# Top-k attention and a hardswish feed-forward: one reciprocal for two pairs of heads, keys and queries transposed by the DMA crossbar, shorter last chains

## The chip, the cores and the metric

The kernel runs on one core of a Trainium2 chip. The metric is device time in microseconds of that core, median of three runs. A core has TensorE (matmuls), VectorE, ScalarE and GpSimd, each with its own in-order stream of instructions, and SyncE (SP), whose queue issues nearly all DMAs. In the profile they are PE (PEld is its weight load), ACT for ScalarE, DVE for VectorE, POOL for GpSimd.

## The reference, cut to what matters

For 8 batches, 8 heads, 576 positions and heads of 64:

```python
scores = scale * q @ k.T
kth = np.partition(scores, -32, axis=-1)[..., -32:-31]
scores = np.where(scores >= kth, scores, -1e9)
attn = exp(scores - max); attn = attn / (sum(attn) + 1e-9)
x = (attn @ v)            # heads side by side: 4608 x 512
h = x @ w_in              # 512 -> 2048
out = (h * clip(h + 3, 0, 6) / 6) @ w_out
```

The two weights arrive as 64-bit floats. The kernel turns each into float32 from its low and high word (`lo`, `hi`).

## The kernel before, in words

**Pairs and duos.** Two heads form a `Pair` (128 partitions wide with keys or queries of both). Two pairs of one batch and one tile of 128 queries form a `Duo`, the unit of the main loop; its two pairs are u=0 and u=1. The 576 queries are four tiles of 128 and a rest of 64; a duo of the rest (`u.rest`, qt = J) has one row a partition and pair instead of two, so half the work. There are 80 duos in 8 batches, 10 a batch: 64 full and 16 rest duos.

**A duo's way.** `scores` (L200) multiplies on TensorE and ScalarE copies the result to SBUF (L233, L236). `top` (L243) finds the 32nd largest of each row on VectorE: four rounds of MAX8 (L250) and, but for the last, MATCH_REPLACE8 (L254). `shift` (L259, GpSimd) makes the bias of the exponential, `exp` (L268, ScalarE) masks with a Prelu, exponentiates with a running sum `den`, and adds EPS to it (L283). `inverse` (L285) is a reciprocal on VectorE. `weights` (L289, GpSimd) multiplies by it (L297) and splits the words of the float32 result into 16-bit halves (L306). `flip` (L309) transposes these by the DMA crossbar from SP. `join` (L314) puts the halves together again as eT (ScalarE for u=0, GpSimd for u=1, L318). `values` (L326) multiplies by the values on TensorE (L338), and `place` (L347) copies to xT on ScalarE.

**Feed-forward.** When both duos of a tile of queries are placed, `feed_forward` is queued (L442): a block of 128 tokens in 16 pieces, eight of matmuls with w_in (L365) with ScalarE's Relu and copy, and GpSimd's gate (L379, L380), then eight with w_out (L385).

**Order.** The schedule is written out by hand: each engine gets its instructions in program order. The main loop (L564) has eight slots for each duo, one search round of one pair in each, so VectorE's searches are the clock of the program. Dictionaries (`usual`, `behind`, `early`, `soon`, L532 to L545) say at which slot, counted from the duo's own first one, each part stands; what stands at 13 is emitted five slots into the next duo. After the parts, `piece` emits feed-forward pieces: one a slot while any are left, an eighth more from 24 and again from 48 left, and half of it in rest duos (L597). The loop runs three duos past the last search, and then what is left follows.

**Keys and queries.** `Pair.load` brings them in by six DMAs on SP. `Pair.transpose` (L171) makes nine transposes on TensorE into PSUM and four ScalarE copies (L179, L180, L183). The pairs of the next batch are loaded at slot 0 of duos 4 to 7 of a batch and transposed at slot 5 of duos 5 to 8.

**Weights.** `convert` (L96) handles one of 32 chunks of 128 x 512 numbers: DMA to `st`; ScalarE's Abs of the high word into `a` (L108) and a scaled copy of the low word into `y` (L111); GpSimd's clamp (L109); on VectorE a shift of `a` (L117) and the sign put into `y` (L118); GpSimd's integer sum of both (L123). `a` and `y` come from the pool "g" in SBUF, which feed-forward uses too. A chunk a slot is begun, so all of it lies in the first four duos.

Of the kernel before, what the change touches and what calls it, by code (L numbers as in the profile page):

```python
# [9 lines left out]
ALU = mybir.AluOpType  # L10
F32 = mybir.dt.float32
U32 = mybir.dt.uint32
I32 = mybir.dt.int32
U16 = mybir.dt.uint16
# [15 lines left out]
def kernel(  # L30
# [9 lines left out]
    nc = tc.nc  # L40
    P = nc.NUM_PARTITIONS
    B, H, S, D = q.shape
    DM, FF = moe_w_in.shape
    J = S // P
    JP = J * P
    R = S - JP
    NHP = H // 2
    NFC = FF // P
# [8 lines left out]
    kqpool = pool("kq", 14)  # L57
# [5 lines left out]
    gpool = pool("g", 8)  # L63
# [3 lines left out]
    ps_w = pool("ps_w", 3, space=PSUM)  # L67
# [25 lines left out]

    WC = 512

    def convert(dst, src):  # L96

        st = kqpool.tile([P, 2 * WC], U32, tag="kq", name="st")
        nc.sync.dma_start(st[:], src)
        yield
        words = st[:].rearrange("p (n two) -> p n two", two=2)
        lo, hi = words[:, :, 0], words[:, :, 1]
        a = gpool.tile([P, WC], F32, tag="g", name="a")
        y = gpool.tile([P, WC], F32, tag="g", name="y")
        nc.scalar.activation(a[:], hi.bitcast(F32), AF.Abs)  # L108
        nc.gpsimd.tensor_scalar(a[:], a[:], HI_MOST, HI_LEAST, ALU.min, ALU.max)  # L109

        nc.scalar.activation(y[:], lo, AF.Copy, bias=2.0, scale=2.0**-51)  # L111
        yield

        au, yu = a[:].bitcast(U32), y[:].bitcast(U32)
        nc.vector.tensor_scalar(au, au, 3, None, ALU.logical_shift_left)  # L117
        nc.vector.scalar_tensor_tensor(  # L118
            out=yu, in0=hi, scalar=0x80000000, in1=yu,
            op0=ALU.bitwise_and, op1=ALU.bitwise_or,  # L120
        )
        yield
        nc.gpsimd.tensor_tensor(  # L123
            dst.bitcast(I32), a[:].bitcast(I32), y[:].bitcast(I32), ALU.add
        )

    def weight_chunks():
# [11 lines left out]
    class Pair:  # L139
# [3 lines left out]
            self.b, self.hp = b, hp  # L143
            self.vm, self.vr, self.kr = vms[hp], vrs[hp], krs[b % 2 * NHP + hp]

        def load(self):
            h0 = 2 * self.hp
            t = self.landed = kqpool.tile([P, 2 * J + 1, 2, D], F32, tag="kq", name="landed")
            for i, src in enumerate((k, q)):
                for hh in range(2):  # L150
                    nc.sync.dma_start(
                        t[:, i * J : (i + 1) * J, hh, :],
                        src[self.b, h0 + hh, 0:JP, :].rearrange("(p j) d -> p j d", j=J),
                    )
                nc.sync.dma_start(
                    t[i * R : (i + 1) * R, 2 * J, :, :],
                    src[self.b, h0 : h0 + 2, JP:S, :].rearrange("h s d -> s h d"),
                )
# [12 lines left out]
        def transpose(self):  # L171
            kq = kqpool.tile([P, JP + S], F32, tag="kq", name="kq")
            self.kT, self.qT = kq[:, 0:JP], kq[:, JP : JP + S]
            ps = big()
            for j in range(2 * J + 1):
                rows = self.landed[:, j, :, :].rearrange("p h d -> p (h d)")
                nc.tensor.transpose(ps[:, j * P : (j + 1) * P], rows, ident[:])  # L177
            c0 = 2 * JP
            nc.scalar.copy(kq[:, 0:c0], ps[:, 0:c0])  # L179
            nc.scalar.copy(kq[:, c0 : c0 + R], ps[:, c0 + R : c0 + 2 * R])  # L180
            for hh in range(2):
                d = slice(hh * D, (hh + 1) * D)
                nc.scalar.copy(self.kr[d, hh, :], ps[d, c0 : c0 + R])  # L183

    class Duo:

# [81 lines left out]
        def exp(self, u):  # L268

            nt, m = self.nt, self.m[u]  # L270
            for t in range(nt):
                row = self.row(u, t)
                nc.scalar.activation(  # L273
                    row, row, AF.Prelu, bias=m[:, t, TOP_K - 1 : TOP_K], scale=-1.0, alpha=FLAT
                )
            for t in range(nt):
                row = self.row(u, t)
                nc.scalar.activation(  # L278
                    row, row, AF.Exp, bias=self.less[u][:, t : t + 1], scale=-scale / FLAT,
                    accum_out=self.den[:, u, t : t + 1],  # L280
                )
            d = self.den[:, u, 0:nt]
            nc.scalar.activation(d, d, AF.Copy, bias=EPS)  # L283

        def inverse(self, u):  # L285
            d = self.den[:, u, 0 : self.nt]
            nc.vector.reciprocal(d, d)  # L287

        def weights(self, u):  # L289

# [18 lines left out]
        def flip(self, u):  # L309
            t16 = self.t16[u] = kqpool.tile([P, 2 * (2 * J + 1), P], U16, tag="kq", name="t16")  # L310
            n = 2 * self.nb
            nc.sync.dma_start_transpose(t16[:, 0:n, :], self.e16[u][:, 0 : n * P])
# [34 lines left out]
        def place(self):  # L347
            nc.scalar.copy(*self.pv)  # L348
# [55 lines left out]
    duos = []  # L404
    for b in range(B):
        halves = [pairs[b][0:2], pairs[b][2:4]]
        for qt in range(J):
            duos += [Duo(h, qt) for h in halves]


            if qt == (0 if b == B - 1 else J - 1) and not 2 < b < B - 1:
                duos += [Duo(h, J) for h in halves]
            elif 2 < b < B - 1 and qt % 2 == 0:
                duos.append(Duo(halves[qt // 2], J))
    assert J == NHP == 4
    per_batch = 2 * J + 2
    ND = len(duos)
# [68 lines left out]
    def land(count=1):  # L486

        for _ in range(min(count, len(chunks))):
            c = convert(*chunks.pop(0))
            next(c)  # L490
            landing.append(c)

# [17 lines left out]
    def pair_at(m, first):  # L510

        b, at = divmod(m, per_batch)
        return pairs[b + 1][at - first] if b + 1 < B and 0 <= at - first < NHP else None

    first = pairs[0]
    first[0].load()
    land(2)
    first[1].load()
    first[0].transpose()
# [10 lines left out]


    usual = dict(  # L532
        shift0=3, exp0=4, inverse0=9, weights0=10, flip0=12, join0=15,
        shift1=7, exp1=8, inverse1=13, weights1=14, flip1=16, join1=19, values=22, place=23,
    )

    behind = dict(usual, values=25, place=26)
    early = dict(
        shift0=3, exp0=3, inverse0=4, weights0=4, flip0=5, join0=8,
        shift1=7, exp1=7, inverse1=8, weights1=8, flip1=9, join1=12, values=12, place=13,  # L540
    )
    soon = dict(
        shift0=3, exp0=3, inverse0=5, weights0=5, flip0=7, join0=10,
        shift1=7, exp1=7, inverse1=9, weights1=9, flip1=11, join1=14, values=16, place=17,
    )  # L545
    queued = {}
    for m in range(ND):
        for part, at in (early if m < 2 else soon if m >= ND - 2 else behind if per_batch <= m < ND - 4 else usual).items():
            queued.setdefault(8 * m + at, []).append((m, part))

    def parts(slot, late=None):

        for m, part in sorted(queued.get(slot, []), key=lambda x: x[1][:-1] != "shift"):
            if late is not None and (part[:-1] in ("inverse", "weights")) != late:
                continue
            if part == "values":
                values(m)
            elif part == "place":
                place(m)
            else:  # L560
                getattr(duos[m], part[:-1])(int(part[-1]))

    due = 0.0
    for m in range(ND + 3):  # L564
        u = duos[m] if m < ND else None
        for i in range(8):
            if u:
                u.top(i // 4, i % 4)
            if m < 4:
                parts(8 * m + i, False)  # L570
            convert_step()
            if m == 0 and i == 0:
                first[3].load()
            if m == 0 and i in (1, 2):
                first[i + 1].transpose()
            if i == (4 if m == 0 else 1) and m + 1 < ND:
                duos[m + 1].scores()
            if m < 4:
                parts(8 * m + i, True)
            else:  # L580
                parts(8 * m + i)
            if m == 0 and i in (1, 4):
                for p in duos[i // 4].pairs:
                    p.load_values()
            if i == 0:
                p = pair_at(m, 4)
                if p:
                    p.load()
            if i == 3 and u and u.pairs[0].b and 1 <= m % per_batch <= 2:
                for p in duos[m - 1].pairs:  # L590
                    p.load_values()
            if i == 5:
                p = pair_at(m, 5)
                if p:
                    p.transpose()

            due += ((left > 0) + (left >= 24) / 8 + (left >= 48) / 8) / (2 if u and u.rest else 1)  # L597
            piece(int(due))
            due -= int(due)
# [36 lines left out]
```

## Time and profile before

| | us |
|---|---|
| median of 3 runs | 1581.27 (1579.84 to 1582.78) |
| span of the profiled run | 1578.5 |
| busy: PE / DVE / POOL / ACT | 1456.9 / 1466.8 / 1144.5 / 1096.3 |
| MAX8, all (L250) | 816.4 |
| MATCH_REPLACE8, all (L254) | 635.5 |
| reciprocals (L287) | 24.6 in 160 |
| transposes of keys and queries on TensorE (L177) | 41.5 in 288 |

Busy time is the sum of the instructions' durations. Neighbouring instructions of VectorE overlap a little, so what one costs in the stream is read from the starts of its neighbours. In a row of groups stand line, engine, operation, output and input with shapes, count, busy time and mean duration in ns, and at the end the engine's idle time before them and what ended it. In the slices each digit is the busy share, in tenths, of a fortieth of the span. In the chain each line is start, duration, and what ran.

### The profile page before, as it was taken

How to read it: one execution, taken by the hardware profiler on the slowest of the kernel's cores; microseconds unless marked ns; L12 is line 12 of the kernel's file. 1: busy time of each engine (PE TensorE's matmuls, PEld its weight loads, DVE VectorE, ACT ScalarE, POOL GpSimd, SP SyncE). 2: the span in 40 equal slices, each digit the busy share in tenths (PEclk: the TensorE clock that was granted, in tenths of full speed). 3: DMA queues.
4: the chain of work that ended last, by engine and by line, in shares of the span. 5: the costliest groups of instructions: out<-in, count | busy, mean ns of one | idle time of the engine just before them, and what ended most of it. 6: DMA issues, size and time to landing. Idle time of an engine off the chain costs nothing.

```text
span 1578.5 us, 28787 instructions
## 1 busy us (share of the span) xinstructions
PE 1456.9 (92%) x10272; PEld 1039.0 (66%) x10272; DVE 1466.8 (93%) x3105; ACT 1096.3 (69%) x1865; POOL 1144.5 (73%) x1264
## 2 busy tenths in 40 slices
PE   5256799979999999998999999999999999999899
PEld 3153566567767777666777777776777767677675
DVE  6999999999999999999999999999999999999700
ACT  6675777777777777777776786777766787777621
POOL 4868687777867777867687777867687777767841
PEclk9568999989999999999999999999999999999999
DMA  8652543444344543545254543446244443533410
GB/s 236 159 181 45 113 83 81 94 91 97 76 90 89 101 83 76 101 85 119 55 106 76 97 89 82 93 93 116 57 96 87 98 88 74 103 65 68 83 22 14
DMA packets 450319, 144.49 MB, mean 92 GB/s; under 512 B 433280, under 2 KB 441472, under 8 KB 450176
## 3 DMA queue, kind: packets, MB, share of 16 engines
q1 hardware_dynamic: 450176, 142.65, 43.5%
q8 instruction: 81, 1.33, 0.3%
q14 instruction: 62, 0.51, 0.1%
HBM read 45.09 MB, written 9.44 MB: 35 GB/s over the span
## 4 chain that ended last, share of the span: by engine, by line
DVE 51%; PE 35%; POOL 5%; issue 3%; ACT 3%; DMA 1%; SPq 1%; POOLq 0%; ACTq 0%; DVEq 0%
DVE m L250 26%; DVE wk L254 22%; PE h L365 14%; PE acc L385 13%; PE pv L338 4%; PE big L232 3%; POOL e L306 1%; DVE y L118 1%; POOL sc L297 1%; DMA t<-e 1%; POOL eT L318 1%; DVE a L117 1%; PE big L177 1%; ACT sc L278 1%; ACT eT L318 1%
## 5 line engine op out<-in xcount | busy, mean ns | idle before, releaser
L250 DVE MAX8 m<-wk 128x8 f32<-128x576 f32 x864 | 613.1, 746 | 2.2
L385 PE MATMUL acc<-w_out,g 128*128 128x512 f32 x1152 | 516.9, 600 | 14.1 <-POOL g L380 14.1
L365 PE MATMUL h<-xT,w_in 128*128 128x128 f32 x4096 | 485.5, 279 | 17.3 <-ACT xT L348 17.3
L365 PEld LDWEIGHTS h<-xT,w_in 128*128 128x128 f32 x4096 | 475.0, 195 | 39.5 <-issue 18.2
L254 DVE MATCH_REPLACE8 wk<-m,wk 128x576 f32<-128x576 f32 x576 | 423.7, 742 | 0.0
L385 PEld LDWEIGHTS acc<-w_out,g 128*128 128x128 f32 x1152 | 213.6, 191 | 260.4 <-issue 238.6
L297 POOL TENSOR_SCALAR sc<-sc,den 128x576 f32<-128x576 f32 x288 | 213.8, 753 | 229.9 <-DVE den L287 222.7
L306 POOL COPY e<-sc 128x2304 uint16<-128x2304 uint16 (+1 forms) x192 | 320.3, 1678 | 10.2
L278 ACT ACTIVATE sc<-sc,shift 128x576 f32<-128x576 f32 x288 | 220.4, 769 | 40.5 <-POOL shift L266 37.7
L318 ACT COPY eT<-t 128x2304 uint16<-128x2304 uint16 (+1 forms) x82 | 215.9, 2632 | 37.9 <-DMA t<-e 35.3
L273 ACT ACTIVATE sc<-sc,m 128x576 f32<-128x576 f32 x288 | 210.1, 777 | 46.2 <-DVE m L250 46.0
L338 PE MATMUL pv<-eT,vm 128*64 128x128 f32 (+1 forms) x2560 | 164.0, 273 | 57.9 <-ACT eT L318 45.8
L254 DVE MATCH_REPLACE8 wk<-m,sc 128x576 f32<-128x576 f32 x288 | 211.8, 742 | 0.0
L318 POOL COPY eT<-t 128x2304 uint16<-128x2304 uint16 (+1 forms) x78 | 203.8, 2613 | 6.9 <-DMA t<-e 6.5
L338 PEld LDWEIGHTS pv<-eT,vm 128*64 128x64 f32 x2560 | 135.2, 141 | 109.3 <-ACT eT L318 49.7
L250 DVE MAX8 m<-sc 128x8 f32<-128x576 f32 x288 | 203.3, 742 | 2.4 <-ACT sc L236 2.4
L373 ACT ACTIVATE g<-h,three 128x512 f32<-128x512 f32 x144 | 98.5, 684 | 150.0 <-PE h L365 140.6
L380 POOL TENSOR_TENSOR g<-g,hs 128x512 f32<-128x512 f32 x144 | 185.0, 1285 | 12.1 <-POOL g L379 0.2
L233 ACT COPY sc<-big 128x2048 f32<-128x2048 f32 (+1 forms) x65 | 119.3, 1836 | 26.1 <-PE big L232 26.0
L232 PE MATMUL big<-kq 64*128 64x512 f32 x512 | 136.4, 653 | 0.0
L379 POOL TENSOR_SCALAR g<-g 128x512 f32<-128x512 f32 x144 | 89.2, 620 | 62.6 <-ACT g L373 52.4
L395 ACT ACTIVATE o<-acc 128x512 f32<-128x512 f32 x36 | 21.4, 595 | 106.6 <-PE acc L385 106.6
(47 smaller groups left out, 1113.1 us busy)
## 6 DMA issues: line engine op xcount, KB each, us to landing
landed<-in_k_dram SPq DMA_DIRECT2D x64, 128.0 KB, 3.0
landed<-in_q_dram SPq DMA_DIRECT2D x64, 128.0 KB, 3.0
st<-in_moe_w_in_dram SPq DMA_DIRECT2D x16, 512.0 KB, 5.1
vm<-in_v_dram SPq DMA_DIRECT2D x64, 128.0 KB, 2.3
st<-in_moe_w_out_dram SPq DMA_DIRECT2D x16, 512.0 KB, 6.6
out_dram<-o SPq DMA_DIRECT2D x32, 256.0 KB, 2.4
t<-e SPq DMA_TRANSPOSE x160, 4.6
landed<-in_k_dram SPq DMA_DIRECT2D x32, 32.0 KB, 2.8
```

Source lines behind the costliest of these rows:

```text
L232: nc.tensor.matmul(banks[:, 2 * i + hh, :], pr.qT[d, qs], pr.kT[d, :])
L250: nc.vector.max(self.m[u][:, t, 8 * r : 8 * r + 8], self.cur[t])
L254: nc.vector.match_replace(wk, self.m[u][:, t, 8 * r : 8 * r + 8], self.cur[t], LOWEST)
L273: nc.scalar.activation(row, row, AF.Prelu, bias=m[:, t, TOP_K - 1 : TOP_K], scale=-1.0, alpha=FLAT)
L278: nc.scalar.activation(row, row, AF.Exp, bias=self.less[u][:, t : t + 1], scale=-scale / FLAT, accum_out=self.den[:, u, t : t + 1],)
L297: nc.gpsimd.tensor_scalar(row, row, self.den[:, u, t : t + 1], 1.0, ALU.mult, ALU.mult)
L306: nc.gpsimd.tensor_copy(halves[:, :, to : to + c1 - c0], words)
L318: copy(eT[:, 0 : self.nb, :] .rearrange("p c q -> p (c q)") .bitcast(U16) .rearrange("p (x h) -> p h x", h=2), self.t16[u][:, 0 : 2 * self ...
L338: nc.tensor.matmul(pv[hh * D : (hh + 1) * D, u * w : (u + 1) * w], pr.vm[:, hh, c, :] if c < J else pr.vr[:, hh, :], rhs, start=(c == 0), ...
L365: nc.tensor.matmul(h[:, (f - f0) * P : (f - f0 + 1) * P], w_in[:, i, f * P : (f + 1) * P], xT[:, i, :], start=(i == 0), stop=(i == NHP - 1),)
L380: nc.gpsimd.tensor_tensor(g[:], g[:], hs[:], ALU.mult)
L385: nc.tensor.matmul(acc[:], gs[f // nf][:, f % nf * P : (f % nf + 1) * P], w_out[:, f, :], start=(f == 0), stop=(f == NFC - 1),)
```

## The change

It has five parts. **Start:** the first pair's queries are loaded from ScalarE's queue and not SP's. **Conversion:** for the first 16 weight chunks (`early`, those of w_in) the low words go to a PSUM tile, and VectorE reads them from there; its result `ys` is a new tile of "g". **Reciprocal:** in the usual order one reciprocal handles both pairs of a duo; adding EPS is a part of its own (`settle`), and u=0's weights, flip and join move to slots 13, 15 and 18, next to those of u=1. **Last chains:** the last six duos take a shorter order (`soon`), the last one a still shorter one (`last`), and the last batch's rest duos follow its second query tile instead of its first. **Keys and queries:** for batches 1 to 7 TensorE's transposes give way to a split into 16-bit halves on GpSimd, a crossbar transpose from SP and a join by ScalarE's copies, spread over slots of two neighbouring duos; their loads come a duo earlier. It is meant to take work off VectorE and TensorE and to bring the last feed-forward blocks forward.

```diff
-    def convert(dst, src):
+    def convert(dst, src, early):
...
-        y = gpool.tile([P, WC], F32, tag="g", name="y")
+        y = (
+            ps_w.tile([P, WC], F32, tag="w", name="yp")
+            if early
+            else gpool.tile([P, WC], F32, tag="g", name="y")
+        )
...
+        ys = gpool.tile([P, WC], F32, tag="g", name="ys") if early else y
...
-            out=yu, in0=hi, scalar=0x80000000, in1=yu,
+            out=ys[:].bitcast(U32), in0=hi, scalar=0x80000000, in1=yu,
...
-            for i, src in enumerate((k, q)):
+            for i, (src, eng) in enumerate(((k, nc.sync), (q, queue or nc.sync))):
...
+        def split(self):
+            self.e16 = kqpool.tile([P, 2 * (2 * J + 1) * P], U16, tag="kq", name="e16")
+            nc.gpsimd.tensor_copy(
...
+        def flip(self):
+            self.t16 = kqpool.tile([P, 2 * (2 * J + 1), P], U16, tag="kq", name="t16")
+            nc.sync.dma_start_transpose(self.t16[:], self.e16[:])
+        def join(self):
...
+            copy(kq[:, 0:c0], halves[:, :, 0:c0])
+            copy(kq[:, c0 : c0 + R], halves[:, :, c0 + R : c0 + 2 * R])
+            for hh in range(2):
+                d = slice(hh * D, (hh + 1) * D)
+                copy(self.kr[d, hh, :], halves[d, :, c0 : c0 + R])
...
+        def inverse(self, us):
+            d = self.den[:, us[0] : us[-1] + 1, 0 : self.nt]
+            nc.vector.reciprocal(d, d)
+        def settle(self, us):
+            d = self.den[:, us[0] : us[-1] + 1, 0 : self.nt]
             nc.scalar.activation(d, d, AF.Copy, bias=EPS)
...
-            if qt == (0 if b == B - 1 else J - 1) and not 2 < b < B - 1:
+            if qt == (1 if b == B - 1 else J - 1) and not 2 < b < B - 1:
...
-            c = convert(*chunks.pop(0))
+            c = convert(*chunks.pop(0), early=len(chunks) >= NFC)
...
-    first[0].load()
+    first[0].load(nc.scalar)
...
     usual = dict(
-        shift0=3, exp0=4, inverse0=9, weights0=10, flip0=12, join0=15,
-        shift1=7, exp1=8, inverse1=13, weights1=14, flip1=16, join1=19, values=22, place=23,
+        shift0=3, exp0=4, shift1=7, exp1=8, settle01=8, inverse01=13, weights0=13, weights1=14,
+        flip0=15, flip1=16, join0=18, join1=19, values=22, place=23,
     )
...
     soon = dict(
-        shift0=3, exp0=3, inverse0=5, weights0=5, flip0=7, join0=10,
-        shift1=7, exp1=7, inverse1=9, weights1=9, flip1=11, join1=14, values=16, place=17,
+        shift0=3, exp0=4, shift1=7, exp1=8, settle01=8, inverse01=10, weights0=10, weights1=11,
+        flip0=12, flip1=13, join0=15, join1=16, values=18, place=18,
     )
+    last = dict(
+        shift0=3, exp0=3, settle0=3, inverse0=5, weights0=5, flip0=7, join0=10,
+        shift1=7, exp1=7, settle1=7, inverse1=8, weights1=8, flip1=9, join1=11, values=11, place=11,
+    )
...
-        for part, at in (early if m < 2 else soon if m >= ND - 2 else behind if per_batch <= m < ND - 4 else usual).items():
+        if m < 2:
+            when = early
+        elif m == ND - 1:
+            when = last
+        elif m >= ND - 6:
+            when = soon
+        else:
+            when = behind if per_batch <= m < ND - 8 else usual
...
-                p = pair_at(m, 4)
+                p = pair_at(m, 3)
...
-            if i == 5:
-                p = pair_at(m, 5)
+            for at, first_at, part in ((2, 4, "split"), (5, 4, "flip"), (1, 5, "join")):
+                p = pair_at(m, first_at) if i == at else None
                 if p:
-                    p.transpose()
+                    getattr(p, part)()
```

In the order for the first two duos (`early`) the reciprocals stay separate, as in `last`.

More of the change, by code (lines that the diff above doesn't have):

```diff
@@ L123, in convert @@
         nc.gpsimd.tensor_tensor(
-            dst.bitcast(I32), a[:].bitcast(I32), y[:].bitcast(I32), ALU.add
+            dst.bitcast(I32), a[:].bitcast(I32), ys[:].bitcast(I32), ALU.add
         )
@@ L144, in __init__, with load @@
             self.vm, self.vr, self.kr = vms[hp], vrs[hp], krs[b % 2 * NHP + hp]
-        def load(self):
+        def load(self, queue=None):
             h0 = 2 * self.hp
             t = self.landed = kqpool.tile([P, 2 * J + 1, 2, D], F32, tag="kq", name="landed")
-            for i, src in enumerate((k, q)):
+            for i, (src, eng) in enumerate(((k, nc.sync), (q, queue or nc.sync))):
                 for hh in range(2):
-                    nc.sync.dma_start(
+                    eng.dma_start(
                         t[:, i * J : (i + 1) * J, hh, :],
@@ L154, in load @@
                     )
-                nc.sync.dma_start(
+                eng.dma_start(
                     t[i * R : (i + 1) * R, 2 * J, :, :],
@@ L183, in transpose, with copy @@
                 nc.scalar.copy(self.kr[d, hh, :], ps[d, c0 : c0 + R])
+        def split(self):
+            self.e16 = kqpool.tile([P, 2 * (2 * J + 1) * P], U16, tag="kq", name="e16")
+            nc.gpsimd.tensor_copy(
+                self.e16[:].rearrange("p (h x) -> p h x", h=2),
+                self.landed[:]
+                .rearrange("p j h d -> p (j h d)")
+                .bitcast(U16)
+                .rearrange("p (x h) -> p h x", h=2),
+            )
[3 more added lines that the diff above has]
+        def join(self):
+            kq = kqpool.tile([P, JP + S], F32, tag="kq", name="kq")
+            self.kT, self.qT = kq[:, 0:JP], kq[:, JP : JP + S]
+            halves = self.t16[:].rearrange("p (h c) q -> p h (c q)", h=2)
+            def copy(dst, src):
+                nc.scalar.copy(dst.bitcast(U16).rearrange("p (x h) -> p h x", h=2), src)
+            c0 = 2 * JP
+            copy(kq[:, 0:c0], halves[:, :, 0:c0])
[3 more added lines that the diff above has]
+                copy(self.kr[d, hh, :], halves[d, :, c0 : c0 + R])
     class Duo:
@@ L281, in exp @@
                 )
-            d = self.den[:, u, 0:nt]
+        def inverse(self, us):
[3 more added lines that the diff above has]
+            d = self.den[:, us[0] : us[-1] + 1, 0 : self.nt]
             nc.scalar.activation(d, d, AF.Copy, bias=EPS)
-        def inverse(self, u):
-            d = self.den[:, u, 0 : self.nt]
-            nc.vector.reciprocal(d, d)
         def weights(self, u):
@@ L538 @@
     early = dict(
-        shift0=3, exp0=3, inverse0=4, weights0=4, flip0=5, join0=8,
-        shift1=7, exp1=7, inverse1=8, weights1=8, flip1=9, join1=12, values=12, place=13,
+        shift0=3, exp0=3, settle0=3, inverse0=4, weights0=4, flip0=5, join0=8,
+        shift1=7, exp1=7, settle1=7, inverse1=8, weights1=8, flip1=9, join1=12, values=12, place=13,
     )
     soon = dict(
-        shift0=3, exp0=3, inverse0=5, weights0=5, flip0=7, join0=10,
-        shift1=7, exp1=7, inverse1=9, weights1=9, flip1=11, join1=14, values=16, place=17,
+        shift0=3, exp0=4, shift1=7, exp1=8, settle01=8, inverse01=10, weights0=10, weights1=11,
+        flip0=12, flip1=13, join0=15, join1=16, values=18, place=18,
+    )
+    last = dict(
+        shift0=3, exp0=3, settle0=3, inverse0=5, weights0=5, flip0=7, join0=10,
+        shift1=7, exp1=7, settle1=7, inverse1=8, weights1=8, flip1=9, join1=11, values=11, place=11,
     )
@@ L547 @@
     for m in range(ND):
-        for part, at in (early if m < 2 else soon if m >= ND - 2 else behind if per_batch <= m < ND - 4 else usual).items():
+        if m < 2:
[6 more added lines that the diff above has]
+            when = behind if per_batch <= m < ND - 8 else usual
+        for part, at in when.items():
             queued.setdefault(8 * m + at, []).append((m, part))
@@ L553, in parts @@
         for m, part in sorted(queued.get(slot, []), key=lambda x: x[1][:-1] != "shift"):
-            if late is not None and (part[:-1] in ("inverse", "weights")) != late:
+            if late is not None and (part[:7] in ("inverse", "weights")) != late:
                 continue
@@ L559, in parts @@
                 place(m)
+            elif part[:-1] in ("settle0", "inverse0"):
+                getattr(duos[m], part[:-2])((0, 1))
+            elif part[:-1] in ("settle", "inverse"):
+                getattr(duos[m], part[:-1])((int(part[-1]),))
             else:
```

## The prediction

> **What bounds the kernel now.** I read the page's busy totals first, then its slices, then the groups of VectorE, the chain, and the timeline around VectorE's last search.
>
> ```profile
> PE 1456.9 (92%) x10272; PEld 1039.0 (66%) x10272; DVE 1466.8 (93%) x3105; ACT 1096.3 (69%) x1865; POOL 1144.5 (73%) x1264
> ...
> PE   5256799979999999998999999999999999999899
> ...
> DVE  6999999999999999999999999999999999999700
> ```
>
> VectorE and TensorE are equally busy, but not at the same time: VectorE is full from the second slice on and has nothing in the last two, where TensorE is full. So the span is VectorE's stream up to its last search, and then a tail that TensorE runs.
>
> ```profile
> L250 DVE MAX8 m<-wk 128x8 f32<-128x576 f32 x864 | 613.1, 746 | 2.2
> ...
> L118 DVE SCALAR_TENSOR_TENSOR y<-st,y 128x512 uint32<-128x512 uint32 x32 | 30.2, 943 | 0.0
> ...
> L287 DVE RECIPROCAL den<-den 128x2 f32<-128x2 f32 x128 | 19.7, 154 | 7.2 <-ACT den L283 7.0
> ```
>
> The last column, idle time before a group, is almost nothing for the searches. From one duo's first MAX8 to the next is 19.40 us for all of the full duos after the fourth, within 0.1 except near the end, and 11.22 for a rest duo: VectorE waits for nobody. TensorE's scores of the last duo start at 1453.22, a little ahead of VectorE's place for them (second search round of the duo that began at 1452.12). So TensorE, though full, holds up no search.
>
> ```profile
> 1487.06 0.16 DVE L287 RECIPROCAL den<-den 128x2 f32<-128x2 f32 x1
> 1487.13 1.40 DVE L250 MAX8 m<-wk 128x8 f32<-128x576 f32 x2
> ...
> 1489.89 1.41 DVE L250 MAX8 m<-wk 128x8 f32<-128x576 f32 x2
> 1498.04 0.17 DVE L287 RECIPROCAL den<-den 128x2 f32<-128x2 f32 x1 [6.73 <-ACT den L283]
> ```
>
> VectorE's last search ends at 1491.3. A reciprocal lasts 0.16 but delays the next MAX8 by 0.07 only (1487.06 to 1487.13): that is its price in the stream.
>
> ```profile
> 1492.99 2.69 POOL eT L318
> 1495.68 0.04 issue
> 1495.72 2.24 PE pv L338 x20
> 1497.96 4.46 PE h L365 x32
> 1502.42 10.30 PE acc L385 x24
> 1512.72 2.33 PE pv L338 x40
> 1515.05 3.63 PE acc L385 x8
> 1518.68 14.29 PE h L365 x128
> 1532.97 13.74 PE acc L385 x32
> 1546.71 14.29 PE h L365 x128
> 1561.00 13.75 PE acc L385 x32
> ```
>
> This is the tail by the chain. One block of the feed-forward is 14.29 + 13.74 = 28.0 us in 16 pieces, so 1.75 a piece. From 1491.3 to the end are 87.2 us: 4.4 waiting for eT, 42 pieces, the values products, 3.9 for the last output.
>
> [...] L118 reads two SBUF tensors and takes 0.67 to 1.75 us for one shape. [...] after its 4.41 us of idle, 20 matmuls took 2.24, against 2.33 for 40 later. [...] SP takes 0.64 us per issue here.
>
> **The change, part by part.**
>
> Start: first queries go out on ScalarE's queue beside the keys. TensorE waits 1.05 us for them today (transposes of the keys end at 5.63, those of the queries begin at 6.67). At most 1.05 comes back, at least 0; I take 1.0, since two queues save 1.9 us of issue and ScalarE has only its table load until 8.0.
>
> Low words in PSUM, for 16 of the 32 chunks: L118 then reads one SBUF tensor, and no longer meets GpSimd. In the timeline seven of the first sixteen run over the undisturbed 0.68, by 5.5 us together. [...] Net -4.5; ends -7 and 0 (the blocked time may come back in L117, which took up to 1.79).
>
> One reciprocal a duo: 77 of 160 go. In some 62 full duos each is worth 0.07, so -4.3. In rest duos a search already waits for the result before it, and the reciprocal stands in that gap: 0. The waits for den ahead of the old ones, 9.3 less the 6.7 after the last search, were 2.6: -2.6.
>
> What it adds: u=0's weights move from slot 10 to 13, right ahead of u=1's. GpSimd then has 2 x (2 x 0.75 + 2.10) = 7.2 us in a row. Queued behind it is shift of the next duo's u=1 (0.45); ScalarE's Exp waits for that (1.9), and the next joint reciprocal waits for Exp, with all of VectorE's searches behind it. Before a full duo's reciprocal there is room. When the next duo is a rest duo with 1.40 us slots, 2 x 2.42 + 6 x 1.40 = 13.3 us are there, and 7.2 + 0.45 + 1.9 + a gate of 1.9 = 11.5 are needed; from rest to rest duo 11.2 against about 10.8. Those are 12 + 4 places, with margins of 0.4 to 3.6. The old waits at such spots were 0.9 and 1.4. Bounds 0 and 2.0 each; I take 0.3, so +5.
>
> Keys and queries by the crossbar, 28 pairs. TensorE loses nine transposes of together 1.15 us a pair: 32 us, which no search waited for and the tail does not contain (no transposes after batch 7 began). GpSimd gains the split, 28 x 2.10 (the row of the 2304-wide copy) = 59, to 1203 us. ScalarE: from the eT copies of 2304 (2.80) and 1536 (1.93) the same kind of copy costs about 2.5 for 2048, 0.34 for 128, so 3.5 a pair against today's 1.01 + 0.22 + 2 x 0.21 = 1.65: +52, to 1148. SP gets 28 transposes more beside 160, 2.7 us each on its queue, landing in 4.6. The join stands four slots (9.7 us) after the flip, and behind it on ScalarE only work that VectorE wants seven slots later (next scores). All of it lies beside the searches: 0, which is the weakest zero here.
>
> Tail: counting the pieces in program order from the slot after the last search, 42 are left before and 41 after: the rest duos go one qt later and the pacing rule is the same. But values of the last duo now stand at slot 11 instead of 16, with 37 pieces behind them. TensorE reaches them early and waits. Chain after the last search: Prelu, Exp and settle 3.5, reciprocal 0.2, weights 3.6, crossbar 4.6, GpSimd's eT 2.8: 15.0 with gaps. Then the 82.8 us from 1495.72 to the end, less 5 pieces and one values: 82.8 - 8.8 - 2.3 = 71.7. Tail 86.7, against 87.2. Within 84 and 92, as GpSimd's order in it turns out.
>
> Sum: -1.0 - 4.5 - 4.3 - 2.6 + 5 - 0.5 = -7.9; 1581.3 - 7.9 = **1573**.
>
> **Rivals.** (a) TensorE is the bound: it has 35% of the chain and is at 97% between 160 and 1480. Then its 32 us come off: 1549. Against it: VectorE's even 19.40. Chance 0.10. (b) The new waits eat the gain: at 0.8 each the 16 places cost 13, and 1581 stays. For it: the small margins. Chance 0.12. (c) Slower: 2.0 at each of the 16 places is 32 us, less 12.4 won, with the tail as it was: 1601; ScalarE and GpSimd, with 111 us more, could do this too through late scores. For it: GpSimd would be at some 80% of VectorE's stretch and works strictly in order. Against it: today its waits for den alone are 222.7 us idle. Chance 0.18. The forecast, waits of 0 to 0.5, has 0.60.
>
> **How the numbers follow.** Faster is the forecast and (a): 0.70; same is (b): 0.12; slower is (c): 0.18. Low end: no new waits (-5), early gain at its best (-2.5), tail 84 (-2.7), and some relief of (a): 1556. High end: waits of about 1.2 at each place, 1588. (a) at 1549 and the larger part of (c) stay out.
>
> **What would show it.** Last MAX8 near 1484; full duos 19.33 apart; [...] waits of den L287 about 5 us, all near rest duos; TensorE idle some 7 us ahead of the last values product, then 37 pieces; no transposes after batch 0. The forecast is wrong if full duos drift above 19.4, if MAX8 waits for the copies of scores, or if TensorE's pieces after the last search are far from 41.

## The result, and the profile after

The changed kernel takes 1604.95 us (1603.54 to 1608.86), the kernel before 1581.16 in the same runs: ratio 1.0154, 95% interval 1.0134 to 1.0174. It is slower by 23.8 us, where 8 us less had been forecast.

First the page's busy totals and VectorE's slices of the changed kernel:

```profile
PE 1441.3 (90%) x10020; PEld 1021.7 (64%) x10020; DVE 1458.7 (91%) x3028; ACT 1125.8 (70%) x1788; POOL 1193.1 (74%) x1292
...
DVE  6999989999999989999999999999999989989700
```

VectorE and TensorE have less to do than before, and the span is longer all the same: single slices of VectorE show an 8 where there was a 9. The waits of the changed kernel, for VectorE and then for ScalarE (who waited, for whom; us in total, times, longest), say what VectorE stands for:

```profile
DVE den L323 <- ACT den L327: 40.4, 14, 6.3
```

```profile
ACT sc L315 <- POOL shift L303: 211.3, 62, 11.3
```

The same two of the kernel before:

```profile
DVE den L287 <- ACT den L283: 9.3, 4, 6.7
```

```profile
ACT sc L278 <- POOL shift L266: 37.7, 26, 6.8
```

Read from the starts of the searches, the 23.2 us between the two profiled spans are these (rows up to the last search add to 20.3):

| | before | after | |
|---|---|---|---|
| first four duos | to 144.1 | to 136.6 | -7.5 |
| a full duo | 19.40 | 19.34 | 60 x 0.06 = -3.6 |
| waits of VectorE after them, up to the last search | 2.9 | 34.3 | +31.4 |
| last search ends | 1491.3 | 1511.8 | +20.5 |
| tail behind it | 87.2 | 89.9 | +2.7 |

Of the 34.3 us, 28.3 are in six rest duos (counted from 0): 5.1 in duo 9, 2.9 in 19, 4.2 in 29, 5.9 in 47, 6.3 in 67, 3.9 in 75. The last two duos have 2.7. The wait in duo 47, in order of time, first GpSimd's, then ScalarE's, then VectorE's lines of the changed kernel's timeline (start, duration, what; in brackets the idle time ahead and who ended it):

```profile
903.18 2.10 POOL L195 COPY e<-landed 128x2304 uint16<-128x2304 uint16 x1 [6.45 <-issue]
...
912.61 1.48 POOL L337 TENSOR_SCALAR sc<-sc,den 128x576 f32<-128x576 f32 x2
914.15 2.10 POOL L346 COPY e<-sc 128x2304 uint16<-128x2304 uint16 x1
916.23 1.48 POOL L337 TENSOR_SCALAR sc<-sc,den 128x576 f32<-128x576 f32 x2
917.77 2.10 POOL L346 COPY e<-sc 128x2304 uint16<-128x2304 uint16 x1
...
921.88 0.20 POOL L300 TENSOR_TENSOR shift<-m 128x2 f32<-128x2 f32 x1
```

```profile
913.32 1.44 ACT L310 ACTIVATE sc<-sc,m 128x576 f32<-128x576 f32 x2
922.43 0.77 ACT L315 ACTIVATE sc<-sc,shift 128x576 f32<-128x576 f32 x1 [7.67 <-POOL shift L303]
```

```profile
905.38 0.17 DVE L323 RECIPROCAL den<-den 128x4 f32<-128x4 f32 x1
...
924.32 0.18 DVE L323 RECIPROCAL den<-den 128x4 f32<-128x4 f32 x1 [5.90 <-ACT den L327]
```

The joint reciprocal at 905.38 frees the weights, but GpSimd, which stood still for 6.45 us ahead of the split (L195), has two gates, a shift and a join to do first and starts them 7.2 us later, at 912.61. They run for 7.2 us without a break; behind them come a gate and then shift at 921.88. ScalarE has done its Prelu long since and waits 7.67 for shift. Exp and settle take 1.9, and VectorE, whose slots are short in this rest duo, has been at its next joint reciprocal for 5.90 us.

The tail of the changed kernel on TensorE:

```profile
1522.91 1.09 PE L378 MATMUL pv<-eT,vm 128*64 128x128 f32 x16 [1.24 <-ACT eT L358]
1523.84 0.39 PE L378 MATMUL pv<-eT,vr 128*64 128x128 f32 x4
1528.83 1.98 PE L378 MATMUL pv<-eT,vm 128*64 128x128 f32 x16 [4.61 <-POOL eT L358]
```

TensorE waits for the last duo's eT with 37 pieces still behind it, 17.0 us after the last search.

### The profile page after: what moved, and what is told of

It reads as the page before. It is cut to its first block, busy times and chain, and to the rows that moved or that the text cites. A ratio compares the mean times of both kernels' runs of the same rounds, so it can differ in the third digit from the quotient of the medians.

```text
span 1601.8 us, 28114 instructions
## 1 busy us (share of the span) xinstructions
PE 1441.3 (90%) x10020; PEld 1021.7 (64%) x10020; DVE 1458.7 (91%) x3028; ACT 1125.8 (70%) x1788; POOL 1193.1 (74%) x1292
## 5 line engine op out<-in xcount | busy, mean ns | idle before, releaser
L405 PEld LDWEIGHTS h<-xT,w_in 128*128 128x128 f32 x4096 | 477.8, 196 | 66.5 <-ACT xT L388 37.1
L346 POOL COPY e<-sc 128x2304 uint16<-128x2304 uint16 (+1 forms) x192 | 320.4, 1679 | 10.2
L358 POOL COPY eT<-t 128x2304 uint16<-128x2304 uint16 (+1 forms) x78 | 203.7, 2611 | 61.1 <-DMA t<-e 56.2
L337 POOL TENSOR_SCALAR sc<-sc,den 128x576 f32<-128x576 f32 x288 | 212.8, 750 | 46.0 <-DVE den L323 44.8
L378 PE MATMUL pv<-eT,vm 128*64 128x128 f32 (+1 forms) x2560 | 167.9, 277 | 78.5 <-ACT eT L358 56.6
L378 PEld LDWEIGHTS pv<-eT,vm 128*64 128x64 f32 x2560 | 139.1, 143 | 128.9 <-ACT eT L358 67.2
L419 POOL TENSOR_SCALAR g<-g 128x512 f32<-128x512 f32 x144 | 88.8, 616 | 98.9 <-ACT g L413 90.1
L195 POOL COPY e<-landed 128x2304 uint16<-128x2304 uint16 x28 | 58.9, 2104 | 43.1 <-DMA t<-e 26.9
```

Source lines behind the costliest of these rows:

```text
L337: nc.gpsimd.tensor_scalar(row, row, self.den[:, u, t : t + 1], 1.0, ALU.mult, ALU.mult)
L346: nc.gpsimd.tensor_copy(halves[:, :, to : to + c1 - c0], words)
L358: copy(eT[:, 0 : self.nb, :] .rearrange("p c q -> p (c q)") .bitcast(U16) .rearrange("p (x h) -> p h x", h=2), self.t16[u][:, 0 : 2 * self ...
L378: nc.tensor.matmul(pv[hh * D : (hh + 1) * D, u * w : (u + 1) * w], pr.vm[:, hh, c, :] if c < J else pr.vr[:, hh, :], rhs, start=(c == 0), ...
L405: nc.tensor.matmul(h[:, (f - f0) * P : (f - f0 + 1) * P], w_in[:, i, f * P : (f + 1) * P], xT[:, i, :], start=(i == 0), stop=(i == NHP - 1),)
```

## The experiments

Theory W: shift stands in GpSimd's queue behind what the joint reciprocal has bunched there, and the searches wait for it through Exp and the next reciprocal. Rival X: the crossbar's extra work on GpSimd, ScalarE and SP makes the waits by itself. Rival T: the tail. Variants called W2 and J, and a rival L, came up on the way. A wait total below ("waits") is that of VectorE after the fourth duo and ahead of the last search; single waits under 0.3 us are left out. All ratios are against the kernel before.

**Separate reciprocals** (`e1`):

```diff
-        shift0=3, exp0=4, shift1=7, exp1=8, settle01=8, inverse01=13, weights0=13, weights1=14,
-        flip0=15, flip1=16, join0=18, join1=19, values=22, place=23,
+        shift0=3, exp0=4, settle0=4, inverse0=9, weights0=10, flip0=12, join0=15,
+        shift1=7, exp1=8, settle1=8, inverse1=13, weights1=14, flip1=16, join1=19, values=22, place=23,
```

(in `soon` alike, with u=0's at 4, 8, 8, 10 and 13).

> The changed kernel with the two reciprocals of a duo separate again and u=0's weights back at slot 10, all else as changed. Theory W (joint reciprocal: 7.2 us of weights stand on GpSimd ahead of the next duo's shift, Exp waits for it, and the next joint reciprocal holds the searches next to rest duos): of the 34 us of waits at den ahead of the last search nearly all go, so 1605 - 31 = 1574 (1568 to 1580). Rival X (the crossbar's extra work on GpSimd, ScalarE and SP makes the waits, whatever the order of the reciprocals): still above 1594. Rival T (the tail took the time): at most 3 us of the 24 are in the tail, so T would leave it above 1598.

1579.44 us, ratio 0.9993 (0.9985 to 1.0002), waits 4.1. The whole loss is undone with the crossbar, the PSUM words and the last chains still in. Its tail is 90.2. X and T fall as sole causes.

**The joint reciprocal alone** (`e2`), the changed `usual` in the kernel before:

> The kernel before with the joint reciprocal alone (settle at 8, reciprocal and u=0's weights at 13, flips at 15 and 16, joins at 18 and 19; its last two duos as before). W in its plain form: the waits at the pairs of rest duos (4 to 5 us each in four places) and at some single ones come with it, so 1581 + 15 to 25 less 3.6 for the cheaper reciprocals: 1592 to 1603. If waits need both the joint reciprocal and the crossbar's split on GpSimd: 1578 to 1588, with waits at the pairs of rest duos alone. X: 1578.

1582.78 us, ratio 1.0015 (1.0009 to 1.0022), waits 11.6. W in its plain form is too large by a factor of two to three: about a third of the waits come with the joint reciprocal, the rest needs something else of the change too. The third is rough: its runs spread from 1580.60 to 1586.62 us, and the profiled one, which gives the waits, took 1580.77.

**The crossbar alone** (`e3`), `split`, `flip` and `join` of keys and queries in the kernel before:

> The kernel before with keys and queries of batches 1 to 7 by the crossbar alone, its separate reciprocals kept. W: VectorE's stream is as before, 1576 to 1584. X: waits at den or at the copies of scores of 15 us and more, above 1595. If TensorE's 32 us had been on the path: 1549.

1580.51 us, ratio 0.9996 (0.9987 to 1.0005), waits 2.1. GpSimd at 1197.9 us busy, 53 more than before, costs VectorE nothing that shows, and TensorE's relief (1456.9 to 1431.2 us busy) brings nothing.

**Start and PSUM words alone** (`e4`):

> The kernel before with the first queries on ScalarE's queue and the low words of 16 chunks in PSUM, nothing else. The changed kernel's first four duos are 7.3 us shorter in all, so 1581 - 7 = 1574 (1572 to 1577); if the 7.3 us came from the new order of the parts instead, 1581.

1577.55 us, ratio 0.9974 (0.9966 to 0.9983): half of what was expected. Its groups on VectorE, the word step without and with PSUM (count, busy us, mean ns):

```profile
L124 DVE SCALAR_TENSOR_TENSOR y<-st,y 128x512 uint32<-128x512 uint32 x16 | 14.7, 918 | 0.0
L124 DVE SCALAR_TENSOR_TENSOR ys<-st,yp 128x512 uint32<-128x512 uint32 x16 | 10.8, 673 | 0.0
```

All sixteen from PSUM are undisturbed (0.673 us in the mean; in the changed kernel 0.67 to 0.68 each, though GpSimd was at work during twelve of them), and the first four duos end at 139.8, 4.3 earlier. In `e2` they end at 140.7, 3.4 earlier: there a wait of 3.3 for GpSimd's clamp (13.3 in all before, 10.2 in `e2`) is gone. So the 7.5 of the changed kernel are the words and the new order in about equal parts.

**The split's own buffer** (`e5`), in the changed kernel:

```diff
-    kqpool = pool("kq", 14)
+    kqpool = pool("kq", 13)
+    splitpool = pool("split", 1)
...
-            self.e16 = kqpool.tile([P, 2 * (2 * J + 1) * P], U16, tag="kq", name="e16")
+            self.e16 = splitpool.tile([P, 2 * (2 * J + 1) * P], U16, tag="split", name="e16")
```

> The changed kernel with one of the 14 buffers of the pool kq set apart for the 16-bit halves of keys and queries, so that GpSimd's split never has to wait for a crossbar transfer that still reads the buffer. Theory W2 (joint reciprocal and crossbar together: flips come late, the split stalls GpSimd on them, the weights then start late and shift behind them later still): the idle time ahead of the split (43 us) goes, waits at den fall from 34 to some 12 to 18 us: 1605 - 19 = 1586 (1580 to 1592). Rival L (the split's 59 us of work on GpSimd is enough by itself): above 1598.

1597.77 us, ratio 1.0102 (1.0087 to 1.0117), waits 28.6. GpSimd's waits ahead of the split went from 43 to 4.6 us and VectorE's in duos 47 and 67 from 12.2 to 5.0. W2 is right in kind and explains 7 us of time, not 19. Rival L is not decided here, since the time lies 0.2 us below its bound.

**u=1's weights behind the next shift** (`e6`), `weights1=16`, flip 19, join 22, values 25 in the changed kernel:

> The changed kernel with its joint reciprocal, but u=1's weights put behind the next duo's second shift (slot 16; flip 19, join 22, values 25) for all but the first two and last six duos. Theory W (shift stands behind 7.2 us of weights): half of that queue is gone, Exp starts 3.6 us earlier, waits at den ahead of the last search fall below 12 us: 1605 - 24 = 1581 (1576 to 1588). If the waits come from the joint reciprocal's own distance of five slots to settle, whatever GpSimd does: no change, 1600 to 1606.

1603.34 us, ratio 1.0138 (1.0123 to 1.0153), waits 31.8. By its time this is the outcome of the rival, "no change"; the trace shows that much did change. One wait took another's place: ScalarE's for shift fell from 211 to 126.5 us, but weights that late hold the buffer of the scores, as ScalarE's waits show,

```profile
ACT sc L270 <- POOL e L346: 71.1, 39, 3.8
```

and VectorE waits for the copies of scores too (8.4 us of the 31.8). So this run neither confirms W nor clears the distance to settle.

**The last chains alone** (`e7`), in the kernel before with separate reciprocals:

> The kernel before with the last chains alone: rest duos of the last batch one query tile later, the short order for the last six duos (its reciprocals separate) and for the last one. Tails in the runs with this part are 89.9 and 90.2 us, without it 85.7 to 88.0: 1581 + 2.5 = 1583.5 (1581 to 1586). If the part had brought the last blocks forward as meant, below 1575.

1584.96 us, ratio 1.0026 (1.0017 to 1.0035), tail 90.2: the part costs about 4 us by time and 2.9 in the tail. TensorE waits 6.31 for the last eT there.

**The joint reciprocal only where a full duo follows** (`e8`), on `e4`, no crossbar:

```diff
+        alone = m < ND - 4 and not duos[m].rest and not duos[m + 1].rest
+        when = early if m < 2 else soon if m >= ND - 2 else dict(joint if alone else usual)
```

> The kernel before with the start and the low words in PSUM, and the joint reciprocal only for full duos that a full duo follows (not the first two, not the last four); no crossbar, old last chains. First four duos some 7 us shorter, 40 and more full duos 0.06 shorter, no new waits next to rest duos: 1581 - 3.2 - 3.4 - 2.5 = 1572 (1569 to 1575). If the joint reciprocal costs as much away from rest duos as beside them: 1578 and above.

1580.89 us, ratio 0.9999 (0.9991 to 1.0008), waits 11.9, nearly all in duos 19, 29, 47 and 73: my list of places was wrong. By its slots (13 to 26) a duo's weights, crossbar, join and values reach into the third duo after it.

**u=1's join two slots later** (`e9`), `join1=21`, values 24 or 25, in the changed kernel, and **with the split's own buffer too** (`e10`):

> The changed kernel with u=1's join two slots later (21 instead of 19; values 24 or 25), nothing else. Theory J (both crossbar transfers of a duo leave SP one after the other, and in the short slots of a rest duo GpSimd comes to the join before the second has landed; it stands still, and weights and shift with it): GpSimd's 56 us of waits for transfers ahead of eT fall under 20, the waits at den in the second rest duos of a pair (16 us) mostly go, those at duos 47 and 67 (12 us, behind the split) stay: 1605 - 14 = 1591 (1585 to 1596). If GpSimd's plain load sets the waits: 1600 to 1606.

> The changed kernel with both: the later join and the split's own buffer, so that GpSimd hardly ever waits for a transfer. J with W2: waits at den fall from 34 to under 10 us, and what is left of the change is its gain in the first four duos and in the full duos against a tail 2.7 us longer: 1605 - 26 = 1579 (1575 to 1586). If the plain load of GpSimd sets the waits: above 1592.

1618.02 us, ratio 1.0238 (1.0223 to 1.0253), and 1619.12, ratio 1.0245 (1.0230 to 1.0261); waits 49.6 and 50.8. J falls: GpSimd's waits for transfers ahead of eT did not go under 20, they rose from 56.2 to 61.5 and 66.5. The edit did something else besides. Slots 13 and 21 both come five slots after a duo's first, so the join of 2.8 us now stands directly ahead of the 7.2 us of weights. With more work ahead of shift there are 15 us more of waits, as W would have it. `e10` ended where GpSimd's plain load was to show (above 1592), but with the join in that place it can't tell plain load from order.

**The joint reciprocal only where three full duos follow** (`e11`), as `e8` with

```diff
+        alone = m < ND - 4 and not any(u.rest for u in duos[m : m + 4])
```

> The kernel before with start and PSUM words, and the joint reciprocal only for duos whose next three and themselves are full (23 duos). The waits next to rest duos need a late join or late weights from up to three duos back, so they should be as in the kernel before (3 us): 1577.6 of start and words alone, less 2.6 in the first four duos and 23 x 0.06 = 1.4: 1573.5 (1571 to 1576). If joint reciprocals bring waits of their own anywhere: 1577 and above.

1576.20 us, ratio 0.9971 (0.9959 to 0.9982), waits 7.0. Faster than before, but not measurably faster than `e4`.

**Values of the last two duos later** (`e12`), on `e11`, values 19 and place 20:

> As the run before it, with the values of the last two duos at slot 19 and place at 20 (16 and 17 in the kernel before), so that feed-forward pieces stand ahead of the products that wait for eT. TensorE's 4.4 us of idle after the last search go and the tail falls from 87.9 to some 83.5: 4 us below that run, about 1569.5. If the last block's start is set by the chain and not by the pieces ahead of it: the same as that run or slower.

1573.13 us, ratio 0.9958 (0.9941 to 0.9974). Inconclusive against `e11`: the intervals overlap, and the tail is 86.5 against 87.2. TensorE still waited 3.75 us after the last search, now ahead of the second-last duo's products and until ScalarE's copy `hs` of the feed-forward ended at 1492.72. That copy stands in ScalarE's order behind an Exp that waited 4.04 us for shift.

**Shift off GpSimd** (`e13`), in the changed kernel:

```diff
-            nc.gpsimd.tensor_tensor(
-                d[:, 0:nt], m[:, 0:nt, TOP_K - 1], m[:, 0:nt, 0], ALU.subtract
-            )
-            nc.gpsimd.tensor_scalar_mul(d[:, 0:nt], d[:, 0:nt], scale)
+            for t in range(nt):
+                kth = mpool.tile([P, 1], F32, tag="kth", name="kth")
+                nc.scalar.activation(kth[:], m[:, t, TOP_K - 1 : TOP_K], AF.Copy, bias=0.0, scale=scale)
+                nc.scalar.activation(
+                    d[:, t : t + 1], m[:, t, 0:1], AF.Prelu, bias=kth[:], scale=-scale, alpha=1.0
+                )
```

> The changed kernel with shift taken off GpSimd: ScalarE makes the bias itself (two small activations a row set) right ahead of the Prelu, so that Exp no longer depends on anything in GpSimd's queue; all else as changed. Theory W (the searches wait because shift stands behind weights, a gate, a split or a join in GpSimd's order, however GpSimd came to be late): waits at den ahead of the last search fall from 34 to under 8 us, 1605 - 24 = 1581 (1574 to 1588, ScalarE being 96 us busier). If ScalarE's own lateness (joins of keys and queries, eT) or the distance to settle makes them: above 1595.

1581.42 us, ratio 1.0001 (0.9992 to 1.0011), 23.5 below the changed kernel's median. Its waits, of VectorE and of GpSimd:

```profile
DVE den L325 <- ACT den L329: 13.4, 8, 6.3
```

```profile
POOL eT L360 <- DMA t<-e: 149.2, 46, 6.3
```

Of the 13.4, 6.3 lie after the last search and 0.5 in the first duo, so 6.6 count, as expected under 8; with 4.2 us of waits for the copies of scores the waits are 10.7. ScalarE is busier by 117 us (1242.8), and GpSimd stands still for transfers 2.7 times as long as in the changed kernel (56.2). But GpSimd also has 63 us less to do, which could have been the cure instead. The trace says no, for GpSimd is still late. After the reciprocals ahead of the six rest duos with the long waits, weights start 4.5 us late on average, where it was 5.2 in the changed kernel; over all joint reciprocals it is 2.5 against 2.4. VectorE's waits for den in these six duos are 1.5 us all the same, against 28.3. That settles W, which names what the searches wait for, however GpSimd came to be late.

**The joint reciprocal everywhere, with shift on ScalarE** (`e14`), on `e12`:

> The fastest run so far (start and PSUM words, values of the last two duos later; 1573.1) with shift on ScalarE and the joint reciprocal in all duos from the third to the fifth from the end. W: no waits next to rest duos (4.5 us were left), 52 more duos with a joint reciprocal of which some 40 are full at 0.06: 1573 - 3 - 2.4 = 1567.5 (1564 to 1572). If ScalarE at some 76% becomes late itself: 1575 and above.

1570.54 us, ratio 0.9927 (0.9911 to 0.9944): the fastest of all, 11.6 us below the kernel before in the same runs (1582.1). The waits did not fall (8.4 against 4.5 in `e12`), and the last search ends at 1487.5, 2.6 us later than in `e12`. So the gain over `e12`, which the intervals hardly separate, is not the one expected: it is the tail, 82.0. There too shift had been in the way, as told under `e12`. Its TensorE lines around the place where `e12` waited 3.75:

```profile
1490.13 1.88 PE L397 MATMUL acc<-w_out,g 128*128 128x512 f32 x4
1492.54 1.09 PE L350 MATMUL pv<-eT,vm 128*64 128x128 f32 x16 [0.53 <-ACT hs L387]
```

## Why the prediction was wrong

**What bounds the kernel** was right: VectorE's stream and a tail behind it. `e3` shows it best, where TensorE has 26 us less and the time stays.

**Start**, -1.0: wrong, close to 0. The first MAX8 of the changed kernel begins at 13.43 (13.59 before). The queries no longer come late, but the keys do, as the first matmuls before and after show:

```profile
4.54 1.09 PE L177 MATMUL big<-ident,landed 128*128 128x128 f32 x4 [4.54 <-DMA landed<-in_k_dram]
```

```profile
5.66 2.15 PE L184 MATMUL big<-ident,landed 128*128 128x128 f32 x9 [5.66 <-DMA landed<-in_k_dram]
```

With both loads in flight the keys' ends 1.1 us later (5.66 against 4.54). I had counted issue time and not the transfer.

**Low words in PSUM**, -4.5: right in size, -4.3 in `e4`, though two readings behind it were off and partly cancelled. Of the first sixteen steps six, not seven, are disturbed (1.09 to 1.75 us, each with GpSimd at work), by 5.1 us together and not 5.5; the seventh is the seventeenth step. And the net of -4.5 is 5.5 less 1.0 for reading from PSUM, an estimate of mine that no trace had shown and no run shows: 0.673 us a step from PSUM, 0.679 in the median before. The new order took some 3 us more off the first four duos (`e2`), a gain that stands in no term.

**One reciprocal a duo**, -4.3: right, -3.6 in the full duos (19.40 to 19.34). **Old waits**, -2.6: they did not go, they grew.

**The new waits**, +5: the step that failed. Prediction: 7.2 + 0.45 + 1.9 + 1.9 = 11.5 us fit into 13.3 in 12 places, and 10.8 into 11.2 in 4, "I take 0.3". Measured: 34.3 us in twelve waits. The mechanism was the one described, and `e13` shows it; what was mis-sized is the start of the sum. It began at the reciprocal, with GpSimd free. In the timeline above GpSimd is 7.2 us late when the weights begin, and ahead of the six long waits it is 2.2 to 7.4 us late; only in duos 42, 78 and 79 (3.5 us of waits) was it in time. It is late because, in order, it stands still for transfers ahead of u=1's join (6.5 us in all before, 46.6 with the joint reciprocal alone, 56.2 after) and ahead of the split (43 us), and then has 7.2 us of weights to do at once. That late weights make late transfers, and these a late join in the next round, is how I read the timeline; no run shows it alone. The idle 222.7 us of GpSimd waiting for den, which I had held against rival (c), did not stay ahead of the weights:

```profile
POOL sc L297 <- DVE den L287: 222.7, 100, 5.1
```

```profile
POOL sc L337 <- DVE den L323: 44.8, 20, 5.3
```

In `e1` they are 158.6. GpSimd's idle time as a whole hardly fell (434 to 409 us); it moved to the waits for transfers, for gates (52.4 to 90.1) and for the searches. Rival (c) had the size, 2.0 at each of 16 places or 32 us, and 1601. That the total fits is partly luck, since ten of its places together have under 3 us.

**Keys and queries by the crossbar**, 0: right alone (`e3`), wrong together. With the joint reciprocal a part of it belongs to the cause, the split's wait for its buffer: waits 11.6 without it (`e2`), 34.3 with it and the rest of the change. Of these 22.7 the split's buffer is 5.7 (`e5`). How the others divide between the crossbar's traffic on SP, the split's work on GpSimd, the joins on ScalarE and the changed order of the last duos stays open.

**Tail**, -0.5: wrong in size, +2.7. The wait for the last eT came as described; the chain took 17.0 us instead of 15.0, since GpSimd served a gate and the second-last duo's join ahead of the last weights, and from TensorE's restart at 1528.8 to the end are 72.9 us instead of 71.7. By `e7` the part is a loss of about 4 us by itself.

## What to carry to other kernels

When an edit gives the same work a new place on an in-order engine, add up what stands in that queue from the last point where the engine is known to be free, not from the event that releases the work. In duo 47 GpSimd came to the weights 7.2 us after the reciprocal that released them. Idle time of that engine is slack only if it stands ahead of that work; a total over the span says little: GpSimd's went from 434 to 409 us, its waits for den from 222.7 to 44.8. A tiny instruction that the bounding engine waits for did not belong in a queue that also waits for DMA transfers here: shift, of 0.20 and 0.22 us, taken off GpSimd made the changed kernel 23.5 us faster (`e13`). Parts of a change do not add up: the joint reciprocal cost 0.15% in the kernel before (`e2`) and 1.6% on top of the rest of the change (`e1` against the changed kernel). Joint reciprocal and crossbar without the other parts were not run.

## What the runs showed of the hardware

A word step with one operand in PSUM was not slowed while GpSimd was at work: 16 of 16 took 0.67 to 0.68 us in the changed kernel, twelve of them with GpSimd at work. In the kernel before, with both operands in SBUF, eleven of 32 took 1.09 to 1.75, each with GpSimd at work, and the other 21 took 0.67 to 0.69. The PSUM source was no slower for this instruction and shape: 0.673 us in the mean of `e4`, against a median of 0.679 before.

Loading keys and queries from two queues at once did not bring the first product forward: the keys' transposes began 1.1 us later (5.66 against 4.54), those of the queries followed without a wait (1.05 before), and the first search began 0.16 us earlier (13.43 against 13.59).
